# A gated mix of two attentions: q and k in separate rows, phi stored by need, A's half of the output kept in SBUF

## The chip, the cores and the metric

The kernel runs on one NeuronCore of a Trainium2 chip, in one launch. The metric is the device time of one execution in microseconds (us). The core has a matrix engine (TensorE, "PE" in the profile; its weight loads are "PEld"), VectorE ("DVE"), ScalarE ("ACT"), GpSimd ("POOL") and SyncE ("SP"). SP computes nothing: in this kernel it issues every DMA, one after the other. An engine works through its own instructions in the order in which the program lists them, and waits at an instruction until what it needs is there.

## The reference

One input `x` of 2048 tokens by 640 goes through two attentions, A and B, each with 32 heads of 20; a sigmoid of `x` times `gate_w` mixes their outputs token by token. A works in four segments of 512 tokens: inside a segment a causal softmax, and across segments a memory `M` with its normaliser `z`, read through phi of q and written through phi of k. B is a causal softmax over a window of 256 tokens.

```python
phi = lambda t: jnp.where(t > 0, t + 1.0, jnp.exp(t))
...
for s in range(N):                     # A, N = 4 segments
    p = _softmax(logits, axis=-1)
    a_dot = jnp.einsum("bhqk,bhkd->bhqd", p, vs)
    pq = phi(qs)
    num = jnp.einsum("bhld,bhde->bhle", pq, M)
    den = jnp.einsum("bhld,bhd->bhl", pq, z)[..., None] + 1e-6
    o = g * (num / den) + (1.0 - g) * a_dot
    pk = phi(ks)
    M = M + jnp.einsum("bhld,bhle->bhde", pk, vs)
    z = z + jnp.einsum("bhld->bhd", pk)
...
g = _sigmoid((x * gate_w).sum(-1, keepdims=True))
return g * (A(x) @ wo_A) + (1 - g) * (B(x) @ wo_B)
```

So phi of q is needed only where a memory exists (segments 1 to 3), and phi of k only where a later segment reads it (segments 0 to 2).

## The kernel before

**Tiling.** The work is cut into 16 steps `T`: four segments `s`, and in each of them four groups of 16 heads, in the order A's first half, B's first half, A's second, B's second (`head(T)`, line 368; groups 0 and 1 are A, 2 and 3 are B). A step projects q, k and v of its group for its segment and then runs four units `u` of four heads each, 64 units in all.

**The projections** (`plan_qk`, line 504) make q and k together, as 640 rows by 512 tokens, in five tiles `m` of 128 rows. Before the change the rows are ordered by half of the group (8 heads), by dimension of the head, by q or k, by head: 16 rows of 8 q heads and 8 k heads for each dimension. Every tile so holds q and k side by side, and tile 2 also holds the border of the two halves.

Each tile is cut into three bf16 parts whose sum is the f32 value (`plan_parts`, line 448: ScalarE, VectorE, ScalarE, then GpSimd or VectorE; the results are called `hl`), and `qk_store` (line 463) writes them to `dqk` in DRAM, in one DMA, or in two for tile 2. For A, phi of the tile is formed (`phi_neg`, `phi_exp`, `phi_sum`) and stored in f32 by `phi_store` for segments 0 to 2; for segments 1 to 3 it is cut into parts as well, which `phl_store` writes. All of this is done for all 640 rows.

**A unit** reads its heads back from DRAM with the dimension of the head on the partitions: six DMAs by `stack_read` (line 586) into `qst` and `kst`, four by `mem_load` (k's phi) and three by `mem_stack` (parts of q's phi). Then come a first product of q and k for the row maxima (line 610, reduced by VectorE in line 621); the maxima are brought into rows of `qst` by way of DRAM (`dmx`, lines 631 to 652); a second product with the maxima taken off (line 675), the exponential on ScalarE (line 682), the mask on GpSimd (lines 688 and 691), and the product with v (line 705). The result is turned by VectorE into `ot` (line 784), scaled, turned back into a tile `os` (`o_back`, line 817) and stored to `o_dram` (`o_store`, line 821). `ot` and `os` have two buffers each.

**The output** (`plan_out`, line 890) is made in 40 pieces: four segments, A and B, five tiles of 128 output rows. The pieces of the earlier segments are spread over the steps from `T` = 5 on; 10 come after the last step. A piece of A is copied by ScalarE into a tile `ys` (line 858) and stored to a DRAM buffer `ya`; for the piece of B it is loaded again (`y_load`, line 866), VectorE adds B's (line 861), and the sum is stored to `out`.

**The order.** Nothing is issued as it is written. `add` gives every piece of work a due time, an engine, a cost, and the buffers that it makes, changes, fills (`put`) or reads (`get`). `Plan.order` (line 93) goes through them as a scheduler would, taking next what can start first by these costs; DMAs have a cost on SP (`DI`, 0.48) and a modelled time on 16 rings. The order found so is the order of each engine's instructions, SP's included. It is fixed when the program is built, and a change of any cost can move instructions on all engines.

Of the kernel before, what the change touches and what calls it, by code (L numbers as in the profile page):

```python
# [10 lines left out]
F32 = mybir.dt.float32  # L11
F32R = mybir.dt.float32r
BF16 = mybir.dt.bfloat16
# [5 lines left out]
D = 640  # L19
H = 32  # L20
DH = 20
S = 2048
L = 512
NSEG = S // L
NC = D // 128
NSG = 4
QK = 640
VW = 322
VA = 21
VROW = 16 * VA + 11  # L30
# [23 lines left out]
class Plan:  # L54
# [216 lines left out]
def attention(ctx, tc, const, dram, xt, wqk, wv, wo, beta, ident, o_dram, out):  # L271
    nc = tc.nc
# [58 lines left out]
    mst = [stack.tile([128, 16, 32], BF16, name=f"mst{i}") for i in range(2)]  # L331
    qfs = [stack.tile([128, 4, L], BF16, name=f"qfs{i}") for i in range(NF)]
    dqk = [dram.tile([3 * QK, S], BF16, name=f"dqk{i}") for i in range(NSG)]
    dphi = [dram.tile([QK, L], F32, name=f"dphi{i}") for i in range(2)]

    dphq = [dram.tile([3 * QK, L], BF16, name=f"dphq{i}") for i in range(2)]
    dmem = dram.tile([4, 128, 96], BF16, name="dmem")

    def init_m():
# [17 lines left out]
    add = plan.add  # L357
# [1 line left out]
    NT = NSG * NSEG  # L359
    NU = 4 * NT  # L360
    PE, ACT, DVE, POOL, SP = "pe", "act", "dve", "pool", "sp"
    DI, DJ = 0.48, 0.65

    def unit(u):
        T, g = divmod(u, 4)
# [2 lines left out]
    def head(T):  # L368


        return (0, 2, 1, 3)[T % NSG], T // NSG
# [84 lines left out]
        add(t + 3e-5, PD, (1.14, 0.61), part_l, k, mod=[hl], get=[res], port=True)  # L456


    def parts_of(m):

        return [(m // 3, 0, 128, 8 * m - 20 * (m // 3))] if m != 2 else [(0, 0, 64, 16), (1, 64, 64, 0)]

    def qk_store(T, m):
        g, s = head(T)
        d = dqk[g]
        for du, r, n, e in parts_of(m):
            nc.sync.dma_start(bass.AP(tensor=d.tensor, offset=d.offset + (3 * QK // 2 * du + 16 * e) * S + L * s,
                                      ap=[[S, n], [QK // 2 * S, 3], [1, L]]), B["hl", ("m", T, m)][r:r + n])


    def phi_neg(T, m):
# [10 lines left out]

    def phl_store(T, m):
        d = dphq[head(T)[0]]
        for du, r, n, e in parts_of(m):
            nc.sync.dma_start(bass.AP(tensor=d.tensor, offset=d.offset + (3 * QK // 2 * du + 16 * e) * L,
                                      ap=[[L, n], [QK // 2 * L, 3], [1, L]]), B["hl", ("phi", T, m)][r:r + n])

    def phi_store(T, m):
        d = dphi[head(T)[0]]  # L490
        for du, r, n, e in parts_of(m):
            nc.sync.dma_start(bass.AP(tensor=d.tensor, offset=d.offset + (QK // 2 * du + 16 * e) * L,
                                      ap=[[L, n], [1, L]]), B["phi", T, m][r:r + n])

    tiles = []
# [8 lines left out]
    def plan_qk(t, dt, T, m):  # L504
        k = ("m", T, m)
        g, s = head(T)
        plan_gemm(t, dt, k, ("x", s), wqk[g, m])
        t += NC * dt - 0.01
        ph, dk = ("phi", T, m), ("dq", T)
        plan_parts(t + 1e-4, k, k)  # L510
        add(t + 3e-4, SP, 1.1 if m == 2 else DI, qk_store, T, m, put=[dk], get=[("hl", k)], size=3 * 2 ** 17, packet=1024)
        if g < 2:
            add(t + 4e-5, ACT, 0.5, phi_neg, T, m, new=[("phi", 2, ph)], get=[k])
            add(t + 5e-5, ACT, 0.54, phi_exp, T, m, mod=[ph])
            add(t + 6e-5, DVE, 0.61, phi_sum, T, m, get=[k], mod=[ph])
            if s < NSEG - 1:
                add(t + 7e-4, SP, 1.1 if m == 2 else DI, phi_store, T, m, get=[ph],
                    new=[("dphi", 2, ("dphi", T))] if m == 0 else [], put=[("dphi", T)] if m else [], size=2 ** 18)
            if s:
                plan_parts(t + 8e-4, ph, ph)  # L520
                add(t + 1e-3, SP, 1.1 if m == 2 else DI, phl_store, T, m, get=[("hl", ph)],
                    new=[("dphq", 2, ("dphq", T))] if m == 0 else [], put=[("dphq", T)] if m else [], size=3 * 2 ** 17, packet=1024)

    def v_mm(T, b, c):
        if c == 0:
# [60 lines left out]
    def stack_read(u, w, i):  # L586
        T, g, _, s = unit(u)
        dst, d = (qst[u % NQ] if w == 0 else kst[u % NK]), dqk[head(T)[0]]
        b, c = RUNS[w][i]
        n = back(T) if w else 0  # L590
        dst = dst[DH * b:DH * (b + c)]
        nc.sync.dma_start(dst[:, :, WIN - n:] if w else dst, bass.AP(
            tensor=d.tensor, offset=d.offset + (3 * QK // 2 * (g // 2) + 8 * w + 4 * (g % 2)) * S + L * s - n,
            ap=[[16 * S, c * DH], [S, 4], [1, L + n]]))

    def back(T):
        g, s = head(T)
# [112 lines left out]
    def mem_load(u, i):  # L710

        T, g, isb, s = unit(u)
        d = dphi[head(T)[0]]
        nc.sync.dma_start(pks[32 * i:32 * i + DH].rearrange("p (x t) -> p x t", t=32), bass.AP(
            tensor=d.tensor, offset=d.offset + (QK // 2 * (g // 2) + 8 + 4 * (g % 2)) * L + 32 * i,
            ap=[[16 * L, DH], [128, 16], [1, 32]]))

    def mem_stack(u, i):
        T, g, isb, s = unit(u)
        d = dphq[head(T)[0]]  # L720
        b, n = ((0, 3), (3, 2), (5, 1))[i]
        nc.sync.dma_start(qfs[u % NF][DH * b:DH * (b + n)], bass.AP(
            tensor=d.tensor, offset=d.offset + (3 * QK // 2 * (g // 2) + 4 * (g % 2)) * L,
            ap=[[16 * L, n * DH], [L, 4], [1, L]]))

    def mem_read(u):
        T, g, isb, s = unit(u)
# [87 lines left out]
        EN[e].tensor_tensor(out=v[:, 0, :, 0:DH], in0=v[:, 0, :, 0:DH], in1=v[:, 1, :, 0:DH], op=ALU.add)  # L815

    def o_back(u):
        t = B["os", u] = work.tile([128, L], F32, name="os", tag="os")
        nc.vector.transpose(t, B["ot", u][:, 0].rearrange("p b e -> p (b e)"))

    def o_store(u):
        T, g, isb, s = unit(u)
        h0 = 16 * (head(T)[0] % 2) + 4 * g
        nc.sync.dma_start(o_dram[1 if isb else 0][h0:h0 + 4, :, L * s:L * s + L]
                          .rearrange("h e t -> (h e) t"), B["os", u])


    ya = dram.tile([D, S], F32, name="ya")

    def plain(i, s):  # L830

# [22 lines left out]
    def y_out(i, s, m):  # L854
        t = B["y", i, s, m]
        if i == 0:
            t = B["ys", i, s, m] = work.tile([128, L], F32, name="ys", tag="ys")
            nc.scalar.activation(t, B["y", i, s, m], AF.Copy)
        else:
            t = B["ys", i, s, m]  # L860
            nc.vector.tensor_tensor(out=t, in0=t, in1=B["y", i, s, m], op=ALU.add)

    def ys_ring(s, m):
        return (("ys", "ys", "res", "phi", "phi")[m] if s == NSEG - 1 else "ys"), 2

    def y_load(s, m):
        tag = ys_ring(s, m)[0]
        t = B["ys", 1, s, m] = work.tile([128, L], F32, name="ys", tag=tag)
        nc.sync.dma_start(t, ya[128 * m:128 * m + 128, L * s:L * s + L])

    def y_store(i, s, m):
        nc.sync.dma_start((ya, out)[i][128 * m:128 * m + 128, L * s:L * s + L], B["ys", i, s, m])

    def plan_oc(t, i, s, c):
        key, sk = (("oc", i, s), c), ("ost", i, s, c)
# [4 lines left out]
        split(t + 1e-4, "ohl", xpool, NO, L, sk, key)  # L880

    def plan_y(t, i, s, m):
        k, ys = ("y", i, s, m), ("ys", i, s, m)
# [104 lines left out]
    for u in range(NU):  # L988
# [129 lines left out]
```

## Time and profile before

| | |
|---|---|
| median of 3 runs | 1177.7 us (1175.34 to 1183.03) |
| profiled execution, its own time | 1191.22 us |
| its span, first to last instruction | 1189.5 us |
| mean granted TensorE clock | 0.968 |
| HBM read, written | 159.98 MB, 80.03 MB |

The profile shows one execution. "Busy" is the time in which an engine has an instruction in work. The granted clock is the share of TensorE's full rate that the chip allowed, and the DMA share is the mean busy share of the core's 16 DMA engines. A row of waits names the engine and line that stood still, what ended the wait, the total in us, how often, and the longest; for SP, `SPq`, it is the time until the next DMA could be issued. The chain of waits is followed back from the last instruction, at each step to what released it. It passes a line many times, and it shows which work was last to come, not all that was busy.

### The profile page before, as it was taken

Reading aid. Unit: us, or ns where it says so; the run is one execution under the profiler, and the core shown is the slowest. Engines: PE = TensorE matmul, PEld = TensorE weight load, DVE = VectorE, ACT = ScalarE, POOL = GpSimd, SP = SyncE. Lnnn points to the kernel's source line nnn. Section 1 sums busy time; section 2 is a strip of 40 time slices with the busy share of each in tenths; the row PEclk is TensorE's granted clock in tenths of the full one; section 3 lists DMA queues with packets and bytes.
Section 4 is the critical chain, followed back from the end, with each engine's and each line's share of the span. In section 5 each row is a group of like instructions: output and inputs, shape, how many; then the busy total and the mean of one; then the engine's idle time right before and its main releaser. Section 6 shows DMA issues by size and latency. Waiting matters only on the chain.

```text
span 1189.5 us, 25082 instructions
## 1 busy us (share of the span) xinstructions
PE 1104.6 (93%) x8322; PEld 722.5 (61%) x8322; DVE 775.4 (65%) x2647; ACT 711.9 (60%) x1513; POOL 828.9 (70%) x1075
## 2 busy tenths in 40 slices
PE   9778999997899999899899999999998999999997
PEld 7564666664565666556566566655665666666555
DVE  3466877764768767586657667777765675667711
ACT  5237675765646774466664777566745657645651
POOL 9345584787756795479776779678875768756864
PEclk9889999998899999899999999999998999999998
DMA  7887777878879788888888878987867777787634
GB/s 218 135 213 185 201 190 192 205 196 168 241 186 244 195 226 199 216 218 235 172 229 193 249 214 226 234 256 192 230 170 209 203 201 194 207 212 208 194 123 150
DMA packets 241393, 241.67 MB, mean 203 GB/s; under 512 B 80752, under 2 KB 195440, under 8 KB 241264
## 3 DMA queue, kind: packets, MB, share of 16 engines
q1 hardware_dynamic: 241264, 240.07, 77.5%
q8 instruction: 66, 1.08, 0.4%
q14 instruction: 63, 0.52, 0.2%
HBM read 159.98 MB, written 80.03 MB: 202 GB/s over the span
## 4 chain that ended last, share of the span: by engine, by line
PE 31%; DMA 22%; POOL 5%; DVE 3%; ACT 3%; issue 2%; SPq 1%; POOLq 0%; DVEq 0%; ACTq 0%
PE bank L429 12%; DMA qst<-dqk 5%; PE bank L675 5%; PE bank L705 5%; PE bank L610 4%; PE bank L531 4%; DMA kst<-dqk 4%; DMA dqk<-hl 2%; ACT P L682 2%; DMA ys<-ya 2%; DMA xst<-wv 2%; DVE bank L621 1%; DMA qst<-dmx 1%; DMA wst<-wqk 1%; POOL P L688 1%
## 5 line engine op out<-in xcount | busy, mean ns | idle before, releaser
L682 ACT ACTIVATE P<-bank 128x512 f32<-128x512 f32 (+2 forms) x768 | 373.7, 563 | 114.5 <-PE bank L675 100.1
L429 PE MATMUL bank<-xhl,w 128*128 128x512 f32 x1200 | 363.5, 429 | 4.0 <-ACT P L682 1.6
L610 PE MATMUL bank<-kst,qst 120*128 120x384 bf16 (+3 forms) x1024 | 258.7, 316 | 35.5 <-DVE mx L621 16.1
L621 DVE CUSTOM_DVE_ANT_0 bank<-bank,mask_a 128x128 f32<-128x128 f32 (+3 forms) x512 | 237.7, 511 | 78.9 <-PE bank L610 77.4
L621 DVE CUSTOM_DVE_ANT_0 bank<-bank,mask_b 128x384 f32<-128x384 f32 (+2 forms) x512 | 258.7, 551 | 38.0 <-PE bank L610 36.4
L675 PE MATMUL bank<-qst,kst 123*128 123x384 bf16 (+2 forms) x1216 | 235.4, 295 | 29.2 <-DMA qst<-dmx 25.5
L394 POOL TENSOR_TENSOR w<-wst,w 128x640 fp32r<-128x640 f32 x119 | 185.2, 1557 | 97.9 <-ACT w L378 96.3
L429 PEld LDWEIGHTS bank<-xhl,w 128*128 128x128 f32 x1200 | 217.9, 192 | 57.9 <-issue 9.3
L688 POOL TENSOR_SCALAR_AFFINE_SELECT P<-P 128x512 f32<-128x512 f32 x256 | 160.8, 636 | 87.1 <-ACT P L682 82.8
L531 PE MATMUL bank<-wv,xhl 128*128 128x320 f32 (+1 forms) x960 | 197.0, 340 | 2.3 <-DVE mx L621 1.3
L429 PE MATMUL bank<-ohl,w 128*128 128x512 f32 x600 | 180.2, 430 | 5.6 <-POOL ohl L394 3.5
L675 PEld LDWEIGHTS <-kst 123*128 123x128 bf16 x1216 | 92.8, 100 | 134.9 <-issue 73.7
L531 PEld LDWEIGHTS bank<-wv,xhl 128*128 128x128 f32 x960 | 154.9, 194 | 16.0 <-DVE mx L621 3.7
L705 PE MATMUL bank<-P,vau 128*32 128x384 f32 (+3 forms) x2432 | 160.2, 407 | 0.9 <-DVE mx L621 0.5
L610 PEld LDWEIGHTS <-qst 120*128 120x128 bf16 x1024 | 83.0, 99 | 128.2 <-issue 89.8
L446 POOL TENSOR_TENSOR hl<-res,hl 128x512 bf16<-128x512 f32 x110 | 128.0, 1165 | 32.8 <-ACT hl L378 32.5
L621 DVE DVE_READ_ACCUMULATOR2_ANT mx<- 128x1 f32 x1024 | 142.5, 139 | 0.0
L378 ACT ACTIVATE w<-wst 128x640 fp32r<-128x640 f32 x121 | 89.9, 743 | 76.4 <-DMA wst<-wqk 29.2
L429 PEld LDWEIGHTS bank<-ohl,w 128*128 128x128 f32 x600 | 111.2, 194 | 31.1 <-POOL ohl L394 5.9
L784 DVE STREAM_TRANSPOSE ot<-bank 128x512 f32<-128x512 f32 x88 | 62.4, 711 | 97.6 <-PE bank L705 95.3
L705 PEld LDWEIGHTS bank<-P,vau 128*32 128x32 f32 x2432 | 69.1, 109 | 81.0 <-issue 62.9
L378 ACT ACTIVATE hl<-res 128x512 bf16<-128x512 f32 x110 | 69.9, 636 | 40.4 <-DVE res L439 29.3
(73 smaller groups left out, 924.0 us busy)
## 6 DMA issues: line engine op xcount, KB each, us to landing
wst<-wqk SPq DMA_DIRECT2D x80, 320.0 KB
dqk<-hl SPq DMA_DIRECT2D x64, 384.0 KB
o_dram<-os SPq DMA_DIRECT2D x64, 256.0 KB
qst<-dqk SPq DMA_DIRECT2D x64, 240.0 KB
kst<-dqk SPq DMA_DIRECT2D x64, 240.0 KB
wst<-wo SPq DMA_DIRECT2D x41, 320.0 KB
xst<-wv SPq DMA_DIRECT2D x80, 161.0 KB
qst<-dqk SPq DMA_DIRECT2D x64, 160.0 KB
```

The costliest lines, as they stand in the source:

```text
L378: nc.scalar.activation(dst, src, AF.Copy)
L394: EN[e].tensor_tensor(out=t[:, 1], in0=B.pop(src), in1=f(t[:, 0]), op=ALU.subtract)
L429: nc.tensor.matmul(p, w[:, a, col:col + 128], x[:, b], start=(c == 0 and i == 0), stop=(c == NC - 1 and i == 2))
L446: EN[e].tensor_tensor(out=t[:, 2], in0=B["res", k], in1=t[:, 1], op=ALU.subtract)
L531: nc.tensor.matmul(p[:, :n], x[:, a, 128 * b:128 * b + 128], w[:, bb, :n], start=(c == 0 and i == 0), stop=(c == NC - 1 and i == 2))
L610: nc.tensor.matmul(pt[:, :n], qst[u % NQ][0:6 * DH, h, 128 * b:128 * b + 128], kst[u % NK][0:6 * DH, h, c0:c0 + n], start=True, stop=True)
L621: nc.vector.tensor_tensor_reduce(out=x, in0=x, in1=mk, scale=1.0, scalar=BIG, op0=ALU.add, op1=ALU.max, accum_out=B["M", u][:, j:j + 1])
L675: nc.tensor.matmul(pt[:, c:c + 128 * n], kst[u % NK][0:6 * DH + 3, h, c0:c0 + 128], q[0:6 * DH + 3, h, 128 * q0:128 * (q0 + n)], start=Tru ...
L682: nc.scalar.activation(B["P", u, b][:, 2 * p + r, c0:c1], B["st", u, b, p, r][:, c0:c1], AF.Exp, scale=SCALE)
L688: nc.gpsimd.affine_select(out=v, in_=v, pattern=[[0, 4], [1, 128]], compare_op=ALU.is_ge, fill=0.0, base=0, channel_multiplier=-1)
L705: nc.tensor.matmul(o[32 * j:32 * j + 32, 128 * q0:128 * (q0 + n)], v[:, VA * h:VA * h + 32], t[:, j, c:c + 128 * n], start=(b == 0 and i = ...
L784: nc.vector.transpose(B["ot", u][:, i].rearrange("p b e -> p (b e)"), B["o" if i == 0 else "num", u])
```

## The change

It has three parts. First, the columns of the q and k weights are ordered by half, then q or k, then dimension, then head: blocks of `QB` = 160 rows, q of the first half, k of the first, q of the second, k of the second. Tile 0 is then all q, tile 4 all k, and tiles 1, 2 and 3 hold a border each. `runs_of` cuts a tile into its pieces, and a store issues one DMA for each of them. Second, `phi_store` writes the k rows alone, `phl_store` the parts of the q rows alone, and a tile without rows that are needed forms no phi, or does not cut it into parts. Third, `ys` has five buffers: A's copy stays there, B's piece is added into it, and `ya`, its store and its load are gone. To make room, `o_back` turns a unit's output into the second half of `ot`, and `o_store` stores from there; the tile `os` is gone.

```diff
+QB = 160
...
-    dphi = [dram.tile([QK, L], F32, name=f"dphi{i}") for i in range(2)]
-    dphq = [dram.tile([3 * QK, L], BF16, name=f"dphq{i}") for i in range(2)]
+    dphi = [dram.tile([2 * QB, L], F32, name=f"dphi{i}") for i in range(2)]
+    dphq = [dram.tile([6 * QB, L], BF16, name=f"dphq{i}") for i in range(2)]
...
-    DI, DJ = 0.48, 0.65
+    DI, DJ, SI = 0.48, 0.65, 0.53
...
-    def parts_of(m):
-        return [(m // 3, 0, 128, 8 * m - 20 * (m // 3))] if m != 2 else [(0, 0, 64, 16), (1, 64, 64, 0)]
+    def runs_of(m, kinds=(0, 1)):
+        out, r = [], 0
+        while r < 128:
+            z, at = divmod(128 * m + r, QB)
+            n = min(QB - at, 128 - r)
+            if z % 2 in kinds:
+                out.append((*divmod(z, 2), at, r, n))
+            r += n
+        return out
+
+    def rows_of(m, kind):
+        return sum(z[4] for z in runs_of(m, (kind,)))
...
-        for du, r, n, e in parts_of(m):
-            nc.sync.dma_start(bass.AP(tensor=d.tensor, offset=d.offset + (3 * QK // 2 * du + 16 * e) * S + L * s,
-                                      ap=[[S, n], [QK // 2 * S, 3], [1, L]]), B["hl", ("m", T, m)][r:r + n])
+        for du, w, at, r, n in runs_of(m):
+            nc.sync.dma_start(bass.AP(tensor=d.tensor, offset=d.offset + (3 * QB * (2 * du + w) + at) * S + L * s,
+                                      ap=[[S, n], [QB * S, 3], [1, L]]), B["hl", ("m", T, m)][r:r + n])
...
-        add(t + 3e-4, SP, 1.1 if m == 2 else DI, qk_store, T, m, put=[dk], get=[("hl", k)], size=3 * 2 ** 17, packet=1024)
-        if g < 2:
+        add(t + 3e-4, SP, SI * len(runs_of(m)), qk_store, T, m, put=[dk], get=[("hl", k)], size=3 * 2 ** 17, packet=1024)
+        nk = rows_of(m, 1) if g < 2 and s < NSEG - 1 else 0
+        nq = rows_of(m, 0) if g < 2 and s else 0
+        if nk or nq:
             add(t + 4e-5, ACT, 0.5, phi_neg, T, m, new=[("phi", 2, ph)], get=[k])
             add(t + 5e-5, ACT, 0.54, phi_exp, T, m, mod=[ph])
             add(t + 6e-5, DVE, 0.61, phi_sum, T, m, get=[k], mod=[ph])
...
+        if nk:
+            add(t + 7e-4, SP, SI * len(runs_of(m, (1,))), phi_store, T, m, get=[ph],
+                new=[("dphi", 2, ("dphi", T))] if m == 1 else [], put=[("dphi", T)] if m > 1 else [], size=2048 * nk)
+        if nq:
+            plan_parts(t + 8e-4, ph, ph)
+            add(t + 1e-3, SP, SI * len(runs_of(m, (0,))), phl_store, T, m, get=[("hl", ph)],
+                new=[("dphq", 2, ("dphq", T))] if m == 0 else [], put=[("dphq", T)] if m else [], size=3072 * nq, packet=1024)
...
-            ap=[[16 * S, c * DH], [S, 4], [1, L + n]]))
+            ap=[[8 * S, c * DH], [S, 4], [1, L + n]]))
...
     def o_back(u):
-        t = B["os", u] = work.tile([128, L], F32, name="os", tag="os")
-        nc.vector.transpose(t, B["ot", u][:, 0].rearrange("p b e -> p (b e)"))
+        v = B["ot", u].rearrange("p i b e -> p i (b e)")
+        nc.vector.transpose(v[:, 1], v[:, 0])
...
-            t = B["ys", i, s, m] = work.tile([128, L], F32, name="ys", tag="ys")
+            t = B["ys", s, m] = work.tile([128, L], F32, name="ys", tag="ys", bufs=NC)
             nc.scalar.activation(t, B["y", i, s, m], AF.Copy)
...
         if i:
             add(t, DVE, 0.6, y_out, i, s, m, get=[k], mod=[ys])
+            add(t + 1e-4, SP, DI, y_store, s, m, get=[ys], size=2 ** 18)
         else:
-            add(t, ACT, 0.48, y_out, i, s, m, get=[k], new=[("ys", 2, ys)])
-        add(t + 1e-4, SP, DI, y_store, i, s, m, get=[ys], put=[] if i else [("ya", s, m)], size=2 ** 18)
+            add(t, ACT, 0.48, y_out, i, s, m, get=[k], new=[("ys", NC, ys)])
...
-        if i:
-            add(t, SP, DI, y_load, s, m, new=[ys_ring(s, m) + (("ys", i, s, m),)], get=[("ya", s, m)],
-                size=2 ** 18)
...
-        add(te + 0.15, DVE, 0.64, o_back, u, get=[ok], new=[("os", 2, ("os", u))])
-        add(te + 0.16, SP, DI, o_store, u, get=[("os", u)], put=[("od", int(isb), s, 4 * (head(T)[0] % 2) + g)], size=2 ** 18)
+        add(te + 0.15, DVE, 0.64, o_back, u, mod=[ok])
+        add(te + 0.16, SP, DI, o_store, u, get=[ok], put=[("od", int(isb), s, 4 * (head(T)[0] % 2) + g)], size=2 ** 18)
...
-        qk.append(np.concatenate(cols, 2).transpose(0, 1, 4, 2, 3).reshape(D, QK))
+        qk.append(np.concatenate(cols, 2).transpose(0, 1, 2, 4, 3).reshape(D, QK))
```

`phl_store`, `phi_store`, `mem_load` and `mem_stack` take the new offsets and strides in the same way.

More of the change, by code (lines that the diff above doesn't have):

```diff
@@ L484, in phl_store @@
         d = dphq[head(T)[0]]
-        for du, r, n, e in parts_of(m):
-            nc.sync.dma_start(bass.AP(tensor=d.tensor, offset=d.offset + (3 * QK // 2 * du + 16 * e) * L,
-                                      ap=[[L, n], [QK // 2 * L, 3], [1, L]]), B["hl", ("phi", T, m)][r:r + n])
+        for du, w, at, r, n in runs_of(m, (0,)):
+            nc.sync.dma_start(bass.AP(tensor=d.tensor, offset=d.offset + (3 * QB * du + at) * L,
+                                      ap=[[L, n], [QB * L, 3], [1, L]]), B["hl", ("phi", T, m)][r:r + n])
     def phi_store(T, m):
         d = dphi[head(T)[0]]
-        for du, r, n, e in parts_of(m):
-            nc.sync.dma_start(bass.AP(tensor=d.tensor, offset=d.offset + (QK // 2 * du + 16 * e) * L,
+        for du, w, at, r, n in runs_of(m, (1,)):
+            nc.sync.dma_start(bass.AP(tensor=d.tensor, offset=d.offset + (QB * du + at) * L,
                                       ap=[[L, n], [1, L]]), B["phi", T, m][r:r + n])
@@ L515, in plan_qk @@
             add(t + 6e-5, DVE, 0.61, phi_sum, T, m, get=[k], mod=[ph])
[L516 to L522, printed above, removed]
+        if nk:
[5 more added lines that the diff above has]
+                new=[("dphq", 2, ("dphq", T))] if m == 0 else [], put=[("dphq", T)] if m else [], size=3072 * nq, packet=1024)
     def v_mm(T, b, c):
@@ L592, in stack_read @@
         nc.sync.dma_start(dst[:, :, WIN - n:] if w else dst, bass.AP(
-            tensor=d.tensor, offset=d.offset + (3 * QK // 2 * (g // 2) + 8 * w + 4 * (g % 2)) * S + L * s - n,
-            ap=[[16 * S, c * DH], [S, 4], [1, L + n]]))
+            tensor=d.tensor, offset=d.offset + (3 * QB * (2 * (g // 2) + w) + 4 * (g % 2)) * S + L * s - n,
+            ap=[[8 * S, c * DH], [S, 4], [1, L + n]]))
     def back(T):
@@ L714, in mem_load @@
         nc.sync.dma_start(pks[32 * i:32 * i + DH].rearrange("p (x t) -> p x t", t=32), bass.AP(
-            tensor=d.tensor, offset=d.offset + (QK // 2 * (g // 2) + 8 + 4 * (g % 2)) * L + 32 * i,
-            ap=[[16 * L, DH], [128, 16], [1, 32]]))
+            tensor=d.tensor, offset=d.offset + (QB * (g // 2) + 4 * (g % 2)) * L + 32 * i,
+            ap=[[8 * L, DH], [128, 16], [1, 32]]))
     def mem_stack(u, i):
@@ L722, in mem_stack @@
         nc.sync.dma_start(qfs[u % NF][DH * b:DH * (b + n)], bass.AP(
-            tensor=d.tensor, offset=d.offset + (3 * QK // 2 * (g // 2) + 4 * (g % 2)) * L,
-            ap=[[16 * L, n * DH], [L, 4], [1, L]]))
+            tensor=d.tensor, offset=d.offset + (3 * QB * (g // 2) + 4 * (g % 2)) * L,
+            ap=[[8 * L, n * DH], [L, 4], [1, L]]))
     def mem_read(u):
@@ L824, in o_store @@
         nc.sync.dma_start(o_dram[1 if isb else 0][h0:h0 + 4, :, L * s:L * s + L]
-                          .rearrange("h e t -> (h e) t"), B["os", u])
-    ya = dram.tile([D, S], F32, name="ya")
+                          .rearrange("h e t -> (h e) t"), B["ot", u][:, 1].rearrange("p b e -> p (b e)"))
     def plain(i, s):
@@ L856, in y_out, with y_store @@
         if i == 0:
-            t = B["ys", i, s, m] = work.tile([128, L], F32, name="ys", tag="ys")
+            t = B["ys", s, m] = work.tile([128, L], F32, name="ys", tag="ys", bufs=NC)
             nc.scalar.activation(t, B["y", i, s, m], AF.Copy)
         else:
-            t = B["ys", i, s, m]
+            t = B["ys", s, m]
             nc.vector.tensor_tensor(out=t, in0=t, in1=B["y", i, s, m], op=ALU.add)
[L863 to L872, printed above, removed]
+    def y_store(s, m):
+        nc.sync.dma_start(out[128 * m:128 * m + 128, L * s:L * s + L], B["ys", s, m])
     def plan_oc(t, i, s, c):
@@ L882, in plan_y @@
     def plan_y(t, i, s, m):
-        k, ys = ("y", i, s, m), ("ys", i, s, m)
+        k, ys = ("y", i, s, m), ("ys", s, m)
         if i:
             add(t, DVE, 0.6, y_out, i, s, m, get=[k], mod=[ys])
+            add(t + 1e-4, SP, DI, y_store, s, m, get=[ys], size=2 ** 18)
         else:
-            add(t, ACT, 0.48, y_out, i, s, m, get=[k], new=[("ys", 2, ys)])
-        add(t + 1e-4, SP, DI, y_store, i, s, m, get=[ys], put=[] if i else [("ya", s, m)], size=2 ** 18)
+            add(t, ACT, 0.48, y_out, i, s, m, get=[k], new=[("ys", NC, ys)])
     def plan_out(t, dt, i, s, m, n=NC):
```

## The prediction

> **What bounds the kernel now.** I read the page first, then busy time by stretch, the waits of TensorE, the waits of SP, and last the chain of waits. From the page:
>
> ```profile
> span 1189.5 us, 25082 instructions
> ...
> PE 1104.6 (93%) x8322; PEld 722.5 (61%) x8322; DVE 775.4 (65%) x2647; ACT 711.9 (60%) x1513; POOL 828.9 (70%) x1075
> ...
> q1 hardware_dynamic: 241264, 240.07, 77.5%
> ...
> PE 31%; DMA 22%; POOL 5%; DVE 3%; ACT 3%; issue 2%; SPq 1%; POOLq 0%; DVEq 0%; ACTq 0%
> ```
>
> TensorE is busy for 93% of the span, and the change leaves it every matmul that it has. So all that can be won is the 84.9 us in which it is idle, and what it loses where its clock is lower. The DMA engines come next: 77.5% of their time for 240 MB, and 22% of the chain. By stretches (busy time of PE, PEld, DVE, ACT and POOL, then granted clock, DMA share and GB/s):
>
> ```profile
> 20.00:40.00 20.00, 20.00 (x98) 16.93 (x97) 6.55 (x16) 12.49 (x24) 17.31 (x16) 1.00 0.87 245
> 40.00:110.00 70.00, 53.88 (x410) 34.50 (x413) 43.83 (x177) 25.37 (x57) 26.22 (x34) 0.85 0.80 171
> ...
> 460.00:530.00 70.00, 63.24 (x501) 39.20 (x500) 48.97 (x152) 39.12 (x87) 42.16 (x51) 0.95 0.86 218
> 530.00:600.00 70.00, 63.77 (x463) 42.69 (x462) 45.42 (x159) 46.91 (x97) 58.78 (x77) 0.95 0.84 206
> 600.00:670.00 70.00, 66.55 (x552) 42.94 (x551) 51.37 (x171) 41.42 (x92) 47.18 (x58) 1.00 0.89 229
> ...
> 880.00:950.00 70.00, 62.22 (x431) 39.84 (x431) 41.83 (x148) 37.53 (x87) 41.41 (x52) 0.93 0.71 187
> ...
> 1150.00:1171.00 21.00, 17.89 (x78) 11.47 (x66) 1.68 (x3) 7.86 (x13) 11.96 (x10) 0.95 0.63 199
> ```
>
> The idleness stands in few places: 16.1 us at the start (40 to 110), 16.4 us from 460 to 670, where the DMA share is 0.84 to 0.89, 7.8 us from 880 to 950, 3.1 us of the end. Where TensorE is idle its clock falls as well: 0.95 over 460 to 600 loses 0.05 x 140 = 7.0 us, 0.93 over 880 to 950 loses 4.9 us. The Trainium skill (TensorE: Matmul & The Clock Gate, section "Part 1: The HAM clock gate") says that an idle window of about 3.4 us halves the clock; the trace agrees in that the low clocks stand in the stretches with stalls. By this rule a stall that only shrinks below the window repays some clock besides, an estimated 1.7 us for each; the sum below leaves that out. What TensorE waited for (total us, times, longest):
>
> ```profile
> PE bank L675 <- DMA qst<-dmx: 25.5, 9, 7.8
> PE bank L610 <- DVE mx L621: 16.1, 17, 9.8
> ```
>
> 25.5 us of its idleness ended when the small transfer of a unit's maxima landed. That one is short; what makes it late is the queue in front of it. (The second row is TensorE waiting for VectorE to free its banks, 9.8 us of it at the start.) SP issues every DMA in order, and SP waits too:
>
> ```profile
> SPq L386 <- DMA kst<-dqk: 24.5, 25, 2.1
> ...
> SPq L872 <- ACT ys L858: 21.1, 8, 6.5
> ```
>
> The first row tells most. A load of weights or of x (L386) needs nothing from a stack read, and yet 25 times it could be issued only when one had landed: a bounded number of DMAs is in flight, and a new one needs an old one's place. The second row is SP standing at a store to `ya` until ScalarE has written its tile, with everything later behind it. The DMA view's groups, from first to last, add up to 1357 issues:
>
> ```profile
> wst<-wqk SPq DMA_DIRECT2D x80, 320.0 KB
> ...
> bet<-beta SPq DMA_DIRECT2D x1, 4.0 KB
> ```
>
> So a place in this queue turns over every 1189.5 / 1357 = 0.877 us, which is the price I use for one DMA where SP sets the pace.
>
> **The change part by part.** The issues that it touches, and the two ends of the ring that it lengthens (one row each from the views by tile; least, median and most ns; first and last start in us):
>
> ```profile
> L872 SPq DMA_DIRECT2D ya<-ys x20: 319/342/431, 322.0 to 1160.0; - x20
> L869 SPq DMA_DIRECT2D ys<-ya x20: 319/400/593, 430.5 to 1165.7; - x20
> L492 SPq DMA_DIRECT2D dphi<-phi x36: 319/374/590, 17.4 to 723.0; - x36
> L486 SPq DMA_DIRECT2D dphq<-hl x36: 370/402/1876, 247.3 to 1018.5; - x36
> L467 SPq DMA_DIRECT2D dqk<-hl x96: 370/425/1517, 19.8 to 1080.0; - x96
> L784 DVE STREAM_TRANSPOSE ot<-bank x88: 671/716/718, 99.0 to 1150.8; 128x512 f32<-128x512 f32 x88
> L824 SPq DMA_DIRECT2D o_dram<-os x64: 319/342/1610, 103.3 to 1153.6; - x64
> ```
>
> *A's half stays in SBUF.* 20 stores and 20 loads of 128 x 512 f32 go: 10.5 MB and 20 x 0.342 + 20 x 0.400 = 14.8 us of issue. SP's 21.1 us of standing at L872 goes with them; late next is whatever stood behind, so I count none of it by itself.
>
> *phi.* Of 640 rows, 320 are k and 320 are q. `phi_store` runs in 6 of the 16 T (A's two halves, s below 3): 6 x 320 rows x 2 KB = 3.9 MB less and 24 issues where 36 were. `phl_store` (s above 0) likewise: 6 x 320 x 3 KB = 5.9 MB less, 24 issues for 36. That is 12 x 0.374 + 12 x 0.402 = 9.3 us of issue. The parts of phi are cut once fewer in each of 6 T (tile 4 is all k), and four phi tiles are not formed at all (tile 0 at s = 0, tile 4 at s = 3, for two halves each).
>
> *q and k apart.* Tiles 1 and 3 are cut by a border of 160 rows as tile 2 was before, so `qk_store` issues 8 DMAs per T where it issued 6: 32 more, 32 x 0.425 = 13.6 us of issue, the same bytes. They stand ahead of the stack reads of the next unit. What 32 and 96 rows cost in place of 128 no row shows. The lower end is nothing, and below it there is no gain, since the bytes are the same; the upper end is 32 x 0.877 = 28.1 us, if each takes a place of which TensorE feels all. I take the share that DMA and SP have of the chain, 23%: 13.6 x 0.23 = 3.1 us, as the bytes don't grow and the nearest rows, the 192 KB halves of tile 2 in the same L467 group, keep to its median. The Trainium skill (DMA: Bandwidth & Descriptors, section "Rules for kernel authors") advises against it: two transfers to disjoint partition halves share the same 16 engines and serialize, so one of 128 partitions is better. By that rule the two pieces win nothing from running side by side, and the sum would carry the upper end, 25 us more; the trace has no store in both forms to settle it, so this is the slower rival below.
>
> *The stack reads* have the old pieces and bytes, only a source row's stride of 8 heads instead of 16: bounded by nothing that I can price, taken as zero.
>
> *The output of a unit* is turned within `ot`, and its store now holds `ot`. Units follow each other every (1150.8 - 99.0) / 63 = 16.7 us; a tile of two buffers is wanted again after 33.4 us, and the first store was issued 4.3 us after its turn (103.3 against 99.0). Even a landing of 8 us, as for L492 below, leaves 20 us: no wait, no cost.
>
> *The engines.*
>
> ```profile
> L446 POOL TENSOR_TENSOR hl<-res,hl 128x512 bf16<-128x512 f32 x110 | 128.0, 1165 | 32.8 <-ACT hl L378 32.5
> ```
>
> Six cuttings of phi are 12 POOL passes of this size (14.0 us at 1.165) and 12 of ScalarE; the four phi tiles are 8 more of ScalarE and 4 of VectorE. POOL is at 70% of the span, ScalarE at 60%, VectorE at 65%: what they save is counted at nothing, since it lies beside TensorE's 93%.
>
> *The order.* The planner places every instruction anew with other store prices, so each engine's order shifts a little everywhere. One stall of the size of the largest mid-kernel wait, 7.8 us with 4.9 us of clock, may come or go: -13 to +13 us, taken as zero.
>
> *What TensorE sees of it.* Less are 20.3 of 240 MB, 8.4%, and 32 of 1357 issues. The chain says where that counts:
>
> ```profile
> by line: PE bank L429 12.2%; DMA qst<-dqk 5.3%; PE bank L675 5.2%; PE bank L705 5.1%; PE bank L610 4.4%; PE bank L531 4.1%; DMA kst<-dqk 3.7%; issue 2.1%; DMA dqk<-hl 1.9%; ACT P L682 1.8%; DMA ys<-ya 1.8%; DMA xst<-wv 1.6%; DVE bank L621 1
> ...
> 530.54 8.23 DMA dphi<-phi
> ...
> 576.69 5.19 DMA dphq<-hl
> ```
>
> The loads from `ya` are 1.8% of it, 21.4 us; they go. Of the two phi pieces, 13.4 us, half goes, 6.7 us. Against this stand the 3.1 us of the added stores: 25.0 us off this path. Not all of it reaches the end: the neighbours on the chain are stack reads, which stay, and in 460 to 670 TensorE has only 16.4 us of idleness to give back. I take half, 12.5 us. At the start phi of T = 0 is 320 rows x 2 KB = 0.66 MB less, 2.7 us at the 245 GB/s of 20 to 40, less two more issues of 0.425: 2 us. At the end five stores and five loads of `ya` leave SP's queue, where TensorE has 3.1 us of idleness: 1 to 3 us, taken as 2. Sum: 12.5 + 2 + 2 = 16.5 us. The profiled execution's own time is 1191.2 us for a span of 1189.5, 1.1% above the median of 1177.7. 1189.5 - 16.5 = 1173.0 is a factor of 0.986, and on the median 1161 us.
>
> **The rivals.** *All of it counts.* If the rest of the chain moves up as well, the 25.0 us come in full, with start and end 29, and the 7.0 us of clock lost in 460 to 600 come back: 36 us, 1142 us. For it speaks that idle time and low clock stand where the DMA share is highest; against it, that the stack reads of 5.3% and 3.7% remain.
>
> *Hidden anyway.* TensorE's other work is paced, and the freed places are taken by DMAs that then wait for their own data. Only some of start and end is won: 0 to 4 us, 1174 to 1178 us. For it speaks the 93%; against it, that 25.5 us of waits end in landings.
>
> *The split stores decide (slower).* In every T the two further stores stand on SP in front of the stack reads of the next unit. Each takes a place at 0.877 us: 28 us in all. With the removed transfers hidden, half of that felt gives +14 us, 1192 us, and all of it 1206. It decides once TensorE feels more than about 0.5 us of each added store (16.5 / 32) or once the rest wins nothing. For it speaks that half of the T (B's) have no phi to save and that `ya` does not start before 322 us; against it, that 64 other issues leave the same queue and the DMA engines get 8% less to move.
>
> *The order turns out worse or better* is in the ranges, at 13 us to either side.
>
> **How the numbers follow.** Chances: half counts 0.50 (own range 1150 to 1168), all counts 0.12, hidden 0.22, split stores 0.16. Predicted is 1161 us. The range of 8 in 10 takes in the first, the third and part of the others: 1140 to 1188 us. A measurement of this kernel tells about 1% from no change, that is 1166 to 1189 us. Faster: 0.44 of the first case and 0.12 = 0.56. Same: 0.06 and 0.20 = 0.26. Slower: 0.16 and 0.02 of a worse order = 0.18.
>
> **What would show it.** Right: about 1325 issues, 220 MB and a DMA share near 0.71 on the page; 64 stores to `dqk` become 128 issues in all; no `ya`; SP's wait at L872 for ScalarE gone; PE's waits for `qst<-dmx` below 25.5 us; mean clock above 0.968; L784 still waiting for matmuls alone. Wrong: DMA share down by a tenth with PE's idle time still about 85 us (hidden); larger waits of TensorE for stack reads in B's stretches (split stores); a single new stall of 8 us or more (order); a wait of L784 for a store (the ring of `ot`).

## The result, and the profile after

The changed kernel takes 1176.06 us at the median of 20 runs (1171.17 to 1186.47), the kernel before 1182.29 (1175.34 to 1188.72). The ratio is 0.995, with a 95% interval of 0.993 to 0.9969. So the change is worth 6 us, where 16.5 were forecast: faster, but by half a per cent, which the prediction counted as "same". The two profiled executions lie 19 us apart (1191.2 and 1172.0 us of own time, spans of 1189.5 and 1170.3): the one before took longer than any of the 20 runs timed, the one after is close to the fastest of its own. A pair of profiles alone would have told a story three times too large. Three runs of the kernel before, timed beside E13 and E14 below, took over 1.5% longer than its fastest and are left out of those two ratios.

The page of the changed kernel:

```profile
span 1170.3 us, 25017 instructions
...
PE 1095.5 (94%) x8322; PEld 717.0 (61%) x8322; DVE 780.8 (67%) x2641; ACT 703.7 (60%) x1495; POOL 815.5 (70%) x1063
...
q1 hardware_dynamic: 227952, 219.75, 74.5%
...
PE 58%; DMA 23%; POOL 6%; DVE 5%; SPq 4%; issue 3%; ACT 2%; POOLq 0%; ACTq 0%; DVEq 0%
```

The bytes went as counted: 219.75 MB where 240.07 were, 20.3 less. The DMA engines' share fell from 77.5% to 74.5% only. Per MB they were busy 0.745 x 1170.3 / 219.75 = 3.97 us, and 3.84 before. Either what was taken out was cheaper than what stayed, or the packets of what stayed took longer; the share alone doesn't tell, but E4 below moves the same 219.75 MB at a share of 73.6% in 1141.1 us, 3.82 us per MB. The same stretches as before (busy PE, PEld, DVE, ACT, POOL, granted clock, DMA share, GB/s):

```profile
40.00:110.00 70.00, 55.81 (x447) 36.18 (x447) 43.66 (x175) 28.15 (x63) 28.67 (x38) 0.90 0.80 177
...
460.00:530.00 70.00, 66.39 (x529) 41.67 (x521) 56.54 (x175) 42.96 (x94) 50.21 (x61) 0.98 0.83 209
530.00:600.00 70.00, 64.47 (x511) 43.07 (x512) 41.52 (x138) 43.58 (x90) 51.03 (x70) 0.95 0.77 182
600.00:670.00 70.00, 63.57 (x518) 39.54 (x516) 53.21 (x171) 39.85 (x88) 45.71 (x57) 1.00 0.83 209
...
880.00:950.00 70.00, 62.24 (x400) 38.88 (x400) 43.84 (x154) 40.78 (x93) 44.09 (x52) 0.95 0.86 219
```

The start is better by 1.9 us and its clock rose from 0.85 to 0.90. From 460 to 670 TensorE was idle for 16.4 us and is now for 15.6: the transfers of `ya` left the chain, and hardly anything was won there. 880 to 950 has the same 7.8 us of idleness. What TensorE waited for hints at why:

```profile
PE bank L687 <- DMA qst<-dmx: 28.3, 10, 7.7
PE bank L622 <- DVE mx L633: 9.8, 10, 7.5
```

The wait for the maxima's small transfer was 25.5 us and is 28.3. The prediction held that this transfer is late because of the queue in front of it. A queue with 8.4% less in it ought to have made it earlier. The longest of these waits, 7.7 us, is as long as before, and at the same place of the work. Here is the chain of waits of the changed kernel around it, and SP's timeline just ahead:

```profile
872.64 9.42 DMA dmx<-mt
...
882.13 7.37 DMA qst<-dmx
...
889.54 1.46 PE bank L687 x3
```

```profile
868.88 0.54 SPq L556 DMA_DIRECT2D dz<-zg  x1
...
872.64 0.53 SPq L660 DMA_DIRECT2D dmx<-mt  x1
```

The store of a unit's maxima, 8 KB, took 9.4 us to land. It was issued 3.8 us after `dz<-zg`, the store of the sigmoid gate's input, which the kernel calls z (it is not the memory's normaliser of that name). This store writes 512 single words of 4 bytes to DRAM, and it is issued four times in a run. The kernel before has the same pair, with the store of z itself on the chain:

```profile
877.91 10.66 DMA dz<-zg
...
888.91 8.63 DMA qst<-dmx
```

The DMA records show more. A transfer's end is reported by words of 4 bytes as well: the trace has 17,904 records of 4 bytes on SP's queue, 2,048 of them the words of z, and 16,656 reports of landing, so what remains beside z's words counts the reports to within 5%. Counted per microsecond from the issue at 868.88, from a list of the trace's own DMA records:

```
us after the issue:  0  1  2   3  4  5  6 7 8 9 10 11 12 13 14 15 16
records of 4 bytes: 20 20 12 443 79 11 10 2 1 1  0  1  7 14 15 13 12
```

The 512 words go out in two microseconds. From the seventh microsecond to the eleventh there are five reports in all, where 10 to 20 per microsecond are usual. After the three other issues, too, there are only 0 to 7 per microsecond for some seven microseconds. It is not the reports alone. Behind the words, for 7, 8, 8 and 5 us after the four stores, the DMA engines moved 48, 42, 37 and 24 GB/s, at busy shares of 0.96, 0.78, 0.68 and 0.80; in the three microseconds from the last store's issue on it was 239 GB/s at 0.75. Packets were in work all the time and hardly moved: single ones took up to 6.9 us. SP is held as well, here behind the third of the stores:

```profile
SPq L604 <- DMA dz<-zg: 4.7, 1, 4.7
```

L604 is a read of q or k, which needs nothing of z. But in this trace SP's 1325 DMAs signal eight semaphores in turn, 165 or 166 each, and a DMA waits until the last one on its semaphore has landed. A store that lands late so also stops SP, at the eighth DMA after it at the latest. So the idea to test was this: TensorE's largest stalls stand behind the store of z, not behind bytes, and the change touches neither that store nor its stalls. I call it "scatter" below, and the prediction's idea "queue". The third idea, "order", is that the planner's new order took back part of what the removed work is worth.

SP's own waits moved rather than went:

```profile
SPq L386 <- POOL w L394: 68.2, 41, 7.4
```

Its standing at the copy of `ya` is gone, as forecast. In its place it now stands for 68.2 us at loads of weights, until GpSimd has freed their buffer. This row had 33.8 us before.

### The profile page after: what moved, and what is told of

Its sections match the earlier page's. It is cut to its first block, busy times and chain, and to the rows that moved or that the text cites. A ratio compares the mean times of both kernels' runs of the same rounds, so it can differ in the third digit from the quotient of the medians.

```text
span 1170.3 us, 25017 instructions
## 1 busy us (share of the span) xinstructions
PE 1095.5 (94%) x8322; PEld 717.0 (61%) x8322; DVE 780.8 (67%) x2641; ACT 703.7 (60%) x1495; POOL 815.5 (70%) x1063
## 2 busy tenths in 40 slices
DMA packets 228081, 221.35 MB, mean 189 GB/s; under 512 B 80240, under 2 KB 189168, under 8 KB 227952
## 3 DMA queue, kind: packets, MB, share of 16 engines
q1 hardware_dynamic: 227952, 219.75, 74.5%
## 4 chain that ended last, share of the span: by engine, by line
PE 58%; DMA 23%; POOL 6%; DVE 5%; SPq 4%; issue 3%; ACT 2%; POOLq 0%; ACTq 0%; DVEq 0%
PE bank L429 22%; PE bank L687 10%; PE bank L717 9%; PE bank L622 8%; PE bank L543 8%; DMA qst<-dmx 3%; DMA qst<-dqk 3%; DMA dmx<-mt 3%; DMA xst<-wv 3%; DVE bank L633 3%; DMA kst<-dqk 2%; DMA wst<-wqk 2%; DMA xst<-o_dram 2%; DMA xst<-xt 1%; SPq L604 1%
## 5 line engine op out<-in xcount | busy, mean ns | idle before, releaser
L622 PE MATMUL bank<-kst,qst 120*128 120x384 bf16 (+3 forms) x1024 | 253.1, 312 | 21.1 <-DVE mx L633 9.8
L687 PE MATMUL bank<-qst,kst 123*128 123x384 bf16 (+2 forms) x1216 | 233.0, 291 | 36.7 <-DMA qst<-dmx 28.3
L543 PE MATMUL bank<-wv,xhl 128*128 128x320 f32 (+1 forms) x960 | 189.5, 335 | 1.3 <-POOL wv L394 0.7
L543 PEld LDWEIGHTS bank<-wv,xhl 128*128 128x128 f32 x960 | 152.5, 192 | 12.3 <-DVE mx L633 2.7
L446 POOL TENSOR_TENSOR hl<-res,hl 128x512 bf16<-128x512 f32 x104 | 121.2, 1167 | 30.3 <-ACT hl L378 28.0
L429 PEld LDWEIGHTS bank<-ohl,w 128*128 128x128 f32 x600 | 108.8, 191 | 31.4 <-POOL ohl L394 5.0
L394 POOL TENSOR_TENSOR wv<-xst,wv 128x322 fp32r<-128x322 f32 x79 | 68.3, 877 | 34.6 <-ACT wv L378 32.5
```

The costliest lines, as they stand in the source:

```text
L394: EN[e].tensor_tensor(out=t[:, 1], in0=B.pop(src), in1=f(t[:, 0]), op=ALU.subtract)
L429: nc.tensor.matmul(p, w[:, a, col:col + 128], x[:, b], start=(c == 0 and i == 0), stop=(c == NC - 1 and i == 2))
L446: EN[e].tensor_tensor(out=t[:, 2], in0=B["res", k], in1=t[:, 1], op=ALU.subtract)
L543: nc.tensor.matmul(p[:, :n], x[:, a, 128 * b:128 * b + 128], w[:, bb, :n], start=(c == 0 and i == 0), stop=(c == NC - 1 and i == 2))
L622: nc.tensor.matmul(pt[:, :n], qst[u % NQ][0:6 * DH, h, 128 * b:128 * b + 128], kst[u % NK][0:6 * DH, h, c0:c0 + n], start=True, stop=True)
L687: nc.tensor.matmul(pt[:, c:c + 128 * n], kst[u % NK][0:6 * DH + 3, h, c0:c0 + 128], q[0:6 * DH + 3, h, 128 * q0:128 * (q0 + n)], start=Tru ...
```

## The experiments

Every kernel was timed in five rounds against the kernel before on the same chip; the groups E1 to E4, E5 to E8, E9 to E12, and E13 with E14 had a chip each, so across groups the ratios are compared, not the microseconds. Below, E4, E5, E6, E8, E9, E10, E11, E13 and E14 keep the order of instructions of one of the two kernels on every engine: the planner is given the old entries (E6 adds to them, at no cost), and only what is issued when an entry's turn comes is altered. E2, E3, E7 and E12 let the planner find a new order.

**E1, the changed kernel again.**

> The changed kernel as it is, beside the runs below on one chip: 0.995 of before again, between 0.991 and 0.999. Its profile shows whether TensorE's waits for the maxima's transfer (28.3 us in the first profile, 25.5 before) stay near 28 or scatter from run to run.

0.9953 (0.9925 to 0.9981), and 28.1 us of waits for `qst<-dmx`. The result and the wait repeat.

**E2, only A's half in SBUF,** and **E3, only q, k and phi.** The diff is split: E2 has the edits of `o_back`, `o_store`, `y_out`, `plan_y` and `plan_out`, E3 all the others.

> Only A's half kept in SBUF (no store to ya, no load from it; 10.5 MB and 40 issues less); q, k and phi as before. Theory 'queue' (bytes and places in SP's queue set TensorE's waits): most of the gain is here, 0.990 of before. Theory 'scatter' (what stalls TensorE is the store of the gate z, 512 writes of 4 bytes, behind which no transfer is reported as landed for some 9 us, and neither part touches it): 0.995 to 1.000. Theory 'order' (the new order of the planner is worth as much as the removed work): anything between 0.985 and 1.010.

> Only q and k apart and phi stored by need (9.8 MB less, 8 issues more); ya as before. 'Queue': 0.996 of before. 'Split stores' (the 32 added stores cost TensorE more than 0.5 us each): 1.005 or more. 'Scatter': 0.997 to 1.001. 'Order': anything between 0.985 and 1.010.

E2 1.004 (1.001 to 1.007), E3 1.0084 (1.0056 to 1.0111). Each part by itself makes the kernel slower, and both together make it faster. No theory in which each transfer has a fixed price gives that. E3's value alone would have spoken for the split stores; E9 below tells it apart.

**E4, z stored in rows, on the changed kernel.** A partition's four values are written as one piece of 16 bytes, read back by four DMAs, and brought into the old order by the exponential that follows anyway:

```diff
-        nc.sync.dma_start(bass.AP(tensor=dz[s].tensor, offset=dz[s].offset, ap=[[1, 4], [16, 32], [4, 4]]),
+        nc.sync.dma_start(bass.AP(tensor=dz[s].tensor, offset=dz[s].offset, ap=[[4, 128], [1, 4]]),
                           zg[:, 4 * s:4 * s + 4])
...
-        nc.sync.dma_start(zc[:, s % 2, 0], bass.AP(tensor=dz[s].tensor, offset=dz[s].offset,
-                                                   ap=[[0, 4], [16, 32], [1, 16]]))
+        for j in range(4):
+            nc.sync.dma_start(zr[32 * j:32 * j + 32, s % 2].rearrange("p (a b) -> p a b", b=4), bass.AP(
+                tensor=dz[s].tensor, offset=dz[s].offset, ap=[[4, 32], [128, 4], [1, 4]]))
...
-        nc.scalar.activation(zc[:, s % 2, 0], zc[:, s % 2, 0], AF.Exp, scale=-1.0)
+        nc.scalar.activation(zc[:, s % 2, 0].rearrange("p (b a) -> p a b", a=4),
+                             zr[:, s % 2].rearrange("p (a b) -> p a b", b=4), AF.Exp, scale=-1.0)
```

> The changed kernel, with z stored as 128 rows of 16 bytes in place of 512 single words, read back by four DMAs of 32 rows, and put in its order by ScalarE's exponential; the planner knows nothing of it. 'Scatter': the three largest waits of the middle (6.0, 4.9 and 7.7 us) and the one of 7.5 us at the start go, TensorE's waits for the maxima's transfer fall from 28.3 us to below 15, and the time to 0.975 of before (25 us less than the changed kernel has, 20 us without the clock). 'Queue': 0.995 as the changed kernel, at most 3 us less.

0.9676 (0.9644 to 0.9709), 1143.49 us at the median: 34 us below the changed kernel in E1, more than the 25 us that "scatter" gave, with 2 KB of data in another shape and the order of all engines kept. TensorE's waits in E4:

```profile
PE bank L690 <- DMA qst<-dmx: 7.8, 7, 2.0
PE bank L690 <- DVE mx L636: 5.6, 7, 2.6
```

The 28.3 us are 7.8, and the longest wait is 2.0 us in place of 7.7. The 20 us from the second, third and fourth store of z on, in the changed kernel and then in E4 (the first store lies in the start):

```profile
270.00:290.00 20.00, 14.00 (x97) 8.45 (x97) 11.96 (x49) 6.95 (x17) 11.66 (x18) 0.89 0.78 133
567.00:587.00 20.00, 15.09 (x106) 9.64 (x95) 7.14 (x23) 9.07 (x18) 12.05 (x18) 0.83 0.84 133
868.00:888.00 20.00, 13.83 (x101) 9.15 (x99) 9.12 (x32) 5.74 (x11) 11.94 (x15) 0.96 0.75 141
```

```profile
262.00:282.00 20.00, 20.00 (x135) 12.34 (x134) 17.30 (x68) 13.57 (x32) 16.69 (x24) 1.00 0.80 208
554.00:574.00 20.00, 20.00 (x163) 13.16 (x155) 13.03 (x42) 14.75 (x32) 14.69 (x22) 1.00 0.88 188
843.00:863.00 20.00, 20.00 (x137) 13.17 (x136) 12.43 (x47) 11.53 (x26) 14.30 (x18) 1.00 0.77 216
```

TensorE is busy for 43 of the 60 us in the one and for all 60 in the other, at full clock. The DMA engines' share is about the same, but they move 188 to 216 GB/s where they moved 133 to 141. "Scatter" stands, and "queue" falls for these stalls.

**E11, only the load of z in four pieces,** the store as before, to tell the store from the load.

> The changed kernel with z stored as before in 512 single words, and only its load cut into four DMAs of 32 rows, as in E4. 'Scatter' (the store is the cause): 0.993 to 0.998, TensorE's waits for the maxima's transfer stay near 28 us. If the load was what E4 mended: 0.968 to 0.975.

0.9982 (0.9946 to 1.0017): no gain from the load. It was the store. The waits for the maxima's transfer were 22.2 us, below the 28 that were written down, without any gain in time.

**E8, z in rows on the kernel before.**

> The kernel before in its own order, with z stored as 128 rows of 16 bytes as in E4. 'Scatter' (an independent 3%): 0.965 to 0.978 of before; the change is then worth E4's 0.9676 against this. If the scatter's stalls were what hid the change, this lies above 0.980 and E4 gains more from the change than 0.5%.

0.9724 (0.968 to 0.9768). The store of z costs 2.8% without the change and, by E4 against E1 (0.9676 / 0.9953 = 0.972), 2.8% with it. It neither hid the change nor was touched by it.

**E5, the kernel before in its own order without the transfers of `ya`.** `y_load` and A's `y_store` issue nothing, A's copy has five buffers, the output is turned within `ot`.

> The kernel before in its own order on every engine, with the 20 stores to ya and the 20 loads from it taken out (A's copy stays in SBUF, a unit's output is turned within ot; the planner still counts the old transfers). This prices A's half without a new order. 'Order' (the removed transfers are worth time, and the new order of run E2 gave it back): 0.985 to 0.993 of before, against 1.004 in E2. 'Hidden' (the transfers cost TensorE nothing): 0.998 to 1.002.

0.9941 (0.9913 to 0.9969), or 7.0 us (4 to 10). E2 takes the same transfers out and ends at 1.004. The two differ in their order alone, and that is worth 1.0% (0.6 to 1.4% by the two intervals).

**E6, the changed kernel in its own order with the transfers of `ya` put back.** They were given to the planner at no cost.

> The changed kernel in its own order, with the 20 stores to ya and the 20 loads from it put back (the load refills the same tile; the planner counts them at nothing). 'Order': 1.002 to 1.010 of before, that is 0.7 to 1.5% above the changed kernel. 'Hidden': 0.995, as the changed kernel.

1.0249 (1.0201 to 1.0297), far outside what either theory gave. SP's waits show what I had built:

```profile
SPq L879 <- DMA ya<-ys: 52.3, 20, 5.1
```

At no cost the planner puts each load right behind its own store, and SP stands at it until the store has landed: 20 times, 52.3 us in all. So E6 says nothing of the price of the transfers alone. It shows another thing: the same transfers, with 52 us of SP standing still and everything queued behind it, came out as 0.0296 x 1182 = 35 us of time, where E5 prices them at 7.0 in the places that they had.

**E9, every store of q and k cut in two,** in the changed kernel's order.

> The changed kernel in its own order, with every store of a piece of q and k cut into two of half the rows: 128 issues more, the same bytes, unknown to the planner. 'Split stores' (0.5 us of TensorE or more for each added store): 1.05 of before or more, 64 us above the changed kernel. By the prediction's price (0.425 us of issue, 23% of it on the path): 12.5 us above it, 1.005 to 1.008. 'Hidden': 0.995 to 0.998.

1.0107 (1.0068 to 1.0146), against E1's 0.9953: 0.0154 x 1184 = 18.2 us for 128 issues, 0.14 us each. At this price the 32 that the change adds cost about 4.6 us, by the two intervals 3 to 6. The prediction's 3.1 was at the lower end of that, and the 28.1 of the slower rival is out.

**E10, the unneeded rows of phi stored again,** to scratch memory, in the changed kernel's order.

> The changed kernel in its own order, with the unneeded rows of phi stored again beside the needed ones, to scratch memory (36 issues and 9.2 MB more; unknown to the planner). If the removed phi rows were worth what the prediction counted (half of 6.7 us, and 2 at the start): 1.000 of before, 5 us above the changed kernel. If they are worth as much per byte as ya in E5: 0.999 to 1.003. 'Hidden': 0.995 to 0.997.

1.0037 (1.0007 to 1.0067), against E1's 0.9953 some 10 us; by the two intervals it can be 5 to 15. The page has 227.25 MB against 221.35, so 5.9 MB came back, not 9.2: the tiles without any needed row aren't formed or cut and store nothing. The run also has 36 issues more than the changed kernel, where the change itself took out 24. At E9's 0.14 us, the 36 would be some 5 of the 10 us; how much is left for the bytes no run separates. The 5.4 us that the prediction counted for phi's rows lie at the lower end of the range, so that they are worth more is likely and not shown.

**E7 and E12, another order alone.** Every instruction is that of the kernel before; only a cost in the planner differs.

```diff
-        add(t + 3e-4, SP, 1.1 if m == 2 else DI, qk_store, T, m, put=[dk], get=[("hl", k)], size=3 * 2 ** 17, packet=1024)
+        add(t + 3e-4, SP, 0.53 * (1, 2, 2, 2, 1)[m], qk_store, T, m, put=[dk], get=[("hl", k)], size=3 * 2 ** 17, packet=1024)
```

```diff
-    DI, DJ = 0.48, 0.65
+    DI, DJ = 0.50, 0.65
```

> The kernel before with no instruction added or taken away; only the planner's cost of storing a tile of q and k is that of the changed kernel (0.53 for each of 1, 2, 2, 2, 1 pieces). So only the order differs. 'Order': off by 0.4% or more to either side, outside 0.996 to 1.004. Every other theory: 1.000, between 0.997 and 1.003.

> The kernel before with every instruction it has; the planner's cost of a DMA on SP is 0.50 where it was 0.48, so only the order differs. E2 against E5 differs by 1% by order alone, E7 by 0.15%. 'Order': between 0.985 and 1.012, outside 0.997 to 1.003 more likely than not.

E7 0.9985 (0.9961 to 1.0008), no difference that can be told. E12 1.0077 (1.0044 to 1.011): the same work, with two hundredths of a microsecond on a cost, is slower by 9 us. That is more than the change won. TensorE's waits for `qst<-dmx` are 13.5 us in E7 and 18.9 in E12, against 25.5 in the kernel before, which is faster than E12. The order alone moves this total by 12 us without moving the time with it, so by itself it prices nothing.

**E13, the whole work of the change in the old order.**

> All of the change's work, in the order of the kernel before: the planner gets the old entries and costs, and what the change leaves out issues nothing when its turn comes; 1327 DMA issues as in the changed kernel. 'Order' (the change is worth what its parts are worth at a fixed order, E5's 7 us and E10's 10 us less a quarter of what E9 adds, 4.6 us; the rest went to the new order): 0.986 to 0.992 of before. If the parts do not add up and the order is not the cause: 0.994 to 0.997, as the changed kernel.

0.990 (0.9863 to 0.9937), 1169.41 us at the median and by the ratio 12 us below the kernel before. E13 makes the same 1325 issues as the changed kernel (the 1327 written down were a miscount), moves the same 219.75 MB and does the same arithmetic. It differs from it in the order alone (with the new order the planner also moved two passes from VectorE to ScalarE), and takes off 12 us where the changed kernel takes off 6. By the two intervals the difference is 1 to 11 us: an order that costs something is shown, its size is not known well. Its row for SP at the loads of weights:

```profile
SPq L386 <- POOL w L394: 47.0, 27, 10.1
```

47.0 us where the changed kernel has 68.2. That is a difference between the two orders that the profile shows; that it is the cause of the 6 us was not tried.

**E14, E13 with z in rows.**

> E13 with the store and load of z as in E4. If the scatter and the change's work are independent: E13's ratio times 0.972, that is 0.958 to 0.965 of before. If without the scatter's stalls the transfers are hidden: 0.966 to 0.973, as E4 and E8.

0.9595 (0.9566 to 0.9623), 1130.35 us at the median (1128.53 to 1133.34): the fastest of all. By the ratios this is 48 us below before and 42 below the changed kernel. E13's 0.990 times E8's 0.972 is 0.963, so the two gains are independent within their intervals. Its page:

```profile
span 1131.6 us, 25044 instructions
...
PE 70%; DMA 15%; DVE 5%; POOL 5%; issue 3%; ACT 2%; SPq 1%; POOLq 0%; DVEq 0%; ACTq 0%
```

TensorE has 70% of the chain now, and the DMA engines 15% where they had 23% in the changed kernel.

## Why the prediction was right or wrong, point by point

**What bounds the kernel** was half right. The idle 84.9 us and the low clock are where time can be won: E4 and E14 won it there. But the sentence on which the rest leans, that the maxima's transfer is late because of the queue in front of it, fails. With 8.4% fewer bytes the wait was 28.3 us for 25.5, which alone would say little (E7 has 13.5 with every byte in place); with 2 KB stored in another shape and all bytes kept it was 7.8 and 8.5 (E4, E8), where the profiles with the old store have 13.5 to 37.6. The rows quoted were right, but the idleness does not stand "in few places": the stretches that were named hold 43.4 of the 84.9 us, and 19.7 more lie from 110 to 460, with the second store of z in them. What I didn't ask was which transfer stood in front at the long waits. One look at SP's timeline ahead of the single wait of 7.8 us would have shown `dz<-zg` at 877.91, and the chain of waits had it as a piece of 10.66 us.

**The terms of the sum,** at a fixed order: `ya` was counted at half of 21.4 and 2 more at the end, 12.7 us, and measured at 7.0 (E5, 4 to 10), so it was too high. The phi pieces were counted at half of 6.7 with 2 more at the start, 5.4 us, and measured at some 10 for 5.9 of the 9.8 MB with 36 issues (E10, 5 to 15). The added stores were counted at 3.1 us, halved with the rest to 1.6, and measured at 4.6 (E9, 3 to 6), so they were too low. Together 16.5 us were forecast, and the whole work in the old order won 12 (E13, interval 7 to 16). The forecast of 0.986 lies at the edge of that interval. So the total at a fixed order was about right and a little high, in part by luck: `ya` and the stores were counted too favourably, phi perhaps too low, some of that cancels, and the reason given for all of them, the queue, was not the right one.

**The order** is the step that failed: "-13 to +13 us, taken as zero". The bounds held, the value did not. The changed kernel's own order costs it 6 us against the old one (E13, 1 to 11), half of what its work is worth. E4 and E14 are a second pair of the same work in the new and the old order, without the stalls of z: 0.9676 and 0.9595, or 10 us (4 to 15). E2 lost 1.0% to its order, E12 0.8% with no other change, E7 nothing. In these draws a new order was never clearly better than the one that was there. What in the new order costs the time stays open: SP's wait for GpSimd at the loads of weights is 68.2 us in the new order and 47.0 in the old, 70.7 in E4 and 48.3 in E14, but no run changes it alone. So 16.5 us forecast became 6 in two steps, 4.5 by the terms of the sum and 6 by the order.

**The rivals.** "Hidden anyway" came nearest, and in time by luck: its 1174 to 1178 us hold the measured 1176.06, but they were counted from 1177.7, the median of three runs, where 20 runs gave 1182.29, and its 0 to 4 us of gain don't hold the 6. It is wrong as a mechanism: at a fixed order the transfers were not hidden (E5, E13), and the order took half of the gain back. "All of it counts" falls with E13, 12 us where it gave 36. "The split stores decide" falls with E9, at 0.14 us each where 0.5 was the point. The Trainium skill's rule that stands beside it (DMA: Bandwidth & Descriptors, "Rules for kernel authors": one transfer of 128 partitions rather than two halves) is right in its sign, since 128 more stores of the same bytes did cost 18.2 us. One store more cost 0.14 us, a third of the 0.425 us that its issue takes on SP.

**The ring of `ot`** cost as good as nothing, as counted: its turn (line 796 after) waited for products and once, for 1.0 us, for the store; in E1 it did not wait for the store at all.

**What would show it.** Issues, bytes, the end of `ya` and of SP's wait for ScalarE came as listed. The DMA share came to 0.745 and not 0.71. The mean clock, 0.968 and 0.982 in the two profiles, came "above 0.968" by the draw of the first profile: over the runs of E1 its median is 0.977 for the kernel before and 0.978 for the changed one. The wait for `qst<-dmx` rose, which was the listed sign that something was wrong.

## What to carry to other kernels

When a small transfer is late, look at what was issued just ahead of it before blaming the number of bytes: here four stores of 512 words of 4 bytes cost 2.8%, and 20 MB in long rows 1.0%. Where a planner orders the work anew for every change of a cost, a change and its order are two things: time the new work in the old order as well, and one more order without new work, or a gain of a per cent is lost in the draw. And in a queue that issues in order, a transfer that waits for its own predecessor can cost more than its bytes: 35 us in E6, where the same transfers were worth 7 in E5.

## What the runs showed of the hardware

I had not expected that one store of 2 KB could hold up all other transfers. After 512 words of 4 bytes had gone out, 0 to 7 words of report came per microsecond for some seven microseconds, where 10 to 20 are usual, the DMA engines moved 24 to 48 GB/s at busy shares of 0.68 to 0.96, and a store of 8 KB issued 3.8 us later took 9.4 us. In rows of 16 bytes, 128 of them, the same 2 KB do nothing of the kind: in the same stretches behind E4's four stores the engines moved 189 to 287 GB/s. The Trainium skill (DMA: Bandwidth & Descriptors, "Queues, rings and completion order") says that the report of a landing is written only after every earlier write of that DMA engine, across its queues. By that rule, reports of later transfers would wait for slow small writes ahead of them, and the records agree in the sequence: words first, silence, then reports. It doesn't cover that packets of data stood too, up to 6.9 us each. What holds them, which of the writes are slow, and whether it is the words' size or their number, no run here separates.
